# Attention and Mish FFN on one core: a pair's softmax straight behind its scores, other places for sums and x steps

## The chip, the core and the metric

The kernel runs on one core of one Trainium2 chip. The metric is the device time of one execution in microseconds (us). The core has TensorE (PE, with its weight loads shown apart as PEld), VectorE (DVE), ScalarE (ACT), GpSimd (POOL) and SyncE (SP, which issues nearly all DMAs here). Each takes its own instructions in order.

## The reference

Attention inside chunks of 64 tokens, for 8 heads of 64 columns, then a feed-forward network of 512 to 2048 to 512 over all 4608 tokens, in float32:

```
scores = scale * q_c @ k_c^T ;  scores -= max(scores)
attn   = exp(scores) / (sum(exp(scores)) + 1e-09)
x      = attn @ v_c                    # heads side by side: (4608, 512)
h      = x @ w_in
g      = h * tanh(softplus(h))         # Mish; softplus(h) = h over 20
out    = g @ w_out
```

## The kernel before

Tokens are worked in 18 pairs of 256. Two pairs make a first block of 512 tokens, which runs by itself; the other 16 make four blocks m = 1 to 4 of 1024 tokens, and while block m is in the network, the attention of the four pairs of block m + 1 is done beside it. The products of the network are done by a scheme of Winograd's kind: seven products of quarter matrices instead of eight, with sums of the parts of x (`x_step`: T1 to T4), of w_in (S1 to S4) and of w_out (T1 to T4, made by `t_whole`, `t_sums`, `t_hi`, `t_lo`, `t_store`; called T-matrices here, u = 0 to 7). Each float32 factor is split into a high part of fewer bits and the rest, and three matmuls are done for one.

All order is written by hand (`tc.manual_schedule()`); the order of the calls is the order of each engine's and queue's instructions. Tiles come from rings of buffers, so an instruction also waits until the former user of its buffer is done.

Block 1 runs in `unit` and then `phase_two` (L1140), 16 steps f = 0 to 15 of 12 matmuls: each casts gh on ACT, subtracts gl on DVE (`g_split`), and `X_PACE[f]` x steps follow. At f = 1 it does the scores and maxima of block 3's first pair (`scores_apart`, `max_apart`), at f = 2 the differences (`sub_apart`).

Blocks 2 to 4 (BOTH_FROM = 2 up to QUADS = 4) run in two stages.

First stage, `up_two(m, n)` (L1240) for n = 0 to 3: the pair with number j of block m + 1 is worked beside 14 products, seven kinds k for two units u; h = 2 * k + i counts them from 0 to 13. A product is 6 matmuls of 128 x 512. Behind each product stand its copies, additions and Mish (G11, G12, G21, G22), then `beside(h)` (L1247) with the steps of the attention and of the sums. Products 8 and 9 (k = 4) are copied by ACT at L1307, and products 10 and 11 (k = 5) write the same banks. The attention of a pair: `scores_apart`, `max_apart`, `sub_apart` (in the pair before, at h = 12, 12, 13), `a_exp` (h = 0), `a_inverse` (sums and reciprocals, h = 2), `a_norm` (3), `a_turn` (transposition on DVE, 4), `a_place` and four `a_swap` (copies on ACT, 5 to 9), `a_values` (matmuls with v, 12), `a_raw` (three copies, 12). v comes in four DMAs of 128 KB (`load_v`), q and k of the next pair in two of 512 KB (`load_qk`), on SP's queue with the loads of operands: 256 KB for each product, issued nine products ahead (`load_op`). In block 2 `BUILDS_UP` adds the T-matrices 4 to 7 at places (n, h).

Second stage, `down_all(m)` (L1344): seven types k of eight steps, 56 steps of 12 matmuls. A step makes the operand of the step after next (`operand`: gh cast on ACT at L1329, gl on DVE at L1332), and the sum of one kind (`difference`, `s_one`, `s_three`); in the first four steps after a type one part of its output is copied and added (`keep_wide`, `total_wide`, DVE at L1389), and one x step of the 22 is taken from `todo`. The accumulator banks are X (two banks, and X_a in the bank that the values of the attention use), Y and Z.

The lines that set the places before:

```
1248  at_ = (5, 6) if m == BOTH_FROM else (1, 2)     # s_sums: sums of g, two units
1329  nc.scalar.copy(out=d["gh"], in_=g)
1332  nc.vector.tensor_tensor(out=d["gl"], in0=g, in1=d["gh"].bitcast(F32), op=ALU.subtract)
1449  if k in (2, 4, 5) and todo:
1450      todo.pop(0)()
```

Of the kernel before, what the change touches and what calls it, by code (L numbers as in the profile page):

```python
# [24 lines left out]
def kernel(  # L25
# [1000 lines left out]
    for n in range(NU):  # L1026
        BUILDS_DOWN.setdefault(n + 1, []).append((t_keep, n))
    BUILDS_UP = t_plan(
        (4, [(0, h) for h in (4, 5, 6, 7, 10)]),
        (5, [(0, 8), (0, 10), (0, 11), (1, 1), (1, 5)]),  # L1030
        (6, [(1, h) for h in (4, 7, 10, 11, 13)]),
        (7, [(2, h) for h in (7, 8, 11, 11, 13)]),
    )

    def unit(m, u):
# [104 lines left out]
    def phase_two(m):  # L1140
        after = m < QUADS
        p = first_pair(m)
        todo = []
        if after:
            todo = [lambda n=n: x_step(m + 1, 0, n) for n in range(len(X_STEPS))]
            todo += [lambda: a_raw(first_pair(m + 1) + 3)]
            todo += [lambda n=n: x_step(m + 1, 1, n) for n in range(len(X_STEPS))]
        for f in range(NF):
            d = {}
            if f == 0:  # L1150
                filled(12)
            g_split(d, z_of(f), f"{m}b_{f}", True)
            if f == 0:
                for t in range(TOK // P):
                    filled(3)
                    store(f"{m}a", (p, p + 2), t)
            elif after or f < NF - 1:
                filled(12)
            down((m, 1), f, d)
            for _ in range(X_PACE[f]):  # L1160
                if todo:
                    todo.pop(0)()
            if m == BOTH_FROM - 1:
                run(BUILDS_DOWN, f)
            nxt = first_pair(m + 2)
            if f == 1:
                a_values(nxt - 1)
                scores_apart(nxt, ("h", "h"))
                max_apart(nxt)
            if f == 2:  # L1170
                sub_apart(nxt)

# [61 lines left out]
    def s_sums(u):  # L1236
        s_one(u)
        s_three(u)

    def up_two(m, n):  # L1240
        units = (2 * n, 2 * n + 1)
        xt, yt, vt = flip(m)
# [2 lines left out]
        x, y, v_ = {}, {}, {}  # L1245

        def beside(h):  # L1247
            at_ = (5, 6) if m == BOTH_FROM else (1, 2)
            if h in at_ and n:
                s_sums(2 * n - 2 + at_.index(h))  # L1250
            if m == BOTH_FROM:
                run(BUILDS_UP, (n, h))
            if h in (10, 11) and n == NU // 2 - 1:
                ready.append(operand(0, h - 10))
            if not on:
                return


            if h == 0:
                a_exp(j)  # L1260
            if h == (1 if n else 3):
                load_v(j)
            if h == 2:
                a_inverse(j)
            if h == 3:
                a_norm(j)
            if h == (3 if n else 5) and first_pair(m + 1) + n + 1 < first_pair(QUADS + 1):
                load_qk(j + 1, pool=(ob_p, "ob"))
            if h == 4:
                a_turn(j)  # L1270
            if h == 5:
                a_place(j)
            if h in (6, 7, 8, 9):
                a_swap(j, h - 6)
            more_ = n < 3 or m + 1 < QUADS
            if h == 12:
                a_values(j)
                if more_:
                    scores_apart(j + 1, yt if n < 3 else ("h", "h"))
                a_raw(j, None if n < 3 else ob_p)  # L1280
                if more_:
                    max_apart(j + 1)
            if h == 13 and more_:
                sub_apart(j + 1)

        for k in range(7):
            for i, u in enumerate(units):
# [56 lines left out]
    def down_all(m):  # L1344
# [83 lines left out]
        for i, (k, u) in enumerate(steps_):  # L1428
# [17 lines left out]
            if late:  # L1446
                step, t = late.pop(0)
                step(t)
            if k in (2, 4, 5) and todo:
                todo.pop(0)()  # L1450
            if u == NU - 1 and k in ends_wide:
                late += [(ends_wide[k], t) for t in range(4)]
# [74 lines left out]
```

## Time and profile before

| | |
|---|---|
| time, median of 3 runs (lowest to highest) | 795.51 us (795.15 to 797.99) |
| the profiled execution | 794.95 us, its span 792.9 us |
| PE busy | 774.7 us, 98% |
| PEld busy | 645.1 us, 81% |
| DVE busy | 574.9 us, 73% |
| ACT busy | 500.6 us, 63% |
| DMA | 245 GB/s in the mean |
| granted clock of PE | 1.0 throughout |

The span holds block 2's stages from 299.6 to 387.4 and to 467.2, block 3's to 553.6 and 634.1, block 4's to 710.4 and the end. PE's idle time is small everywhere but at the start, so the busy share tells little; the waits of PE by stretch tell what is left. A wait names the line that waited and, behind the arrow, the line that it waited for. For one wait the row of a matmul and that of its weight load differ, since a matmul's recorded end lies beyond the start of the next one, and weight loads run ahead.

### The profile page before, as it was taken

How to read it: one execution, taken by the hardware profiler on the slowest of the kernel's cores; microseconds unless marked ns; L12 is line 12 of the kernel's file. 1: busy time of each engine (PE TensorE's matmuls, PEld its weight loads, DVE VectorE, ACT ScalarE, POOL GpSimd, SP SyncE). 2: the span in 40 equal slices, each digit the busy share in tenths (PEclk: the TensorE clock that was granted, in tenths of full speed). 3: DMA queues.
4: the chain of work that ended last, by engine and by line, in shares of the span. 5: the costliest groups of instructions: out<-in, count | busy, mean ns of one | idle time of the engine just before them, and what ended most of it. 6: DMA issues, size and time to landing. Idle time of an engine off the chain costs nothing.

```text
span 792.9 us, 15588 instructions
## 1 busy us (share of the span) xinstructions
PE 774.7 (98%) x5850; PEld 645.1 (81%) x5850; DVE 574.9 (73%) x917; ACT 500.6 (63%) x787; POOL 2.2 (0%) x7
## 2 busy tenths in 40 slices
PE   5999999999999999999999999999999999999998
PEld 4887887888788887788888888887888888888887
DVE  6778898755757886777799965565899823348875
ACT  5988986736547447787756657777556444454443
POOL 1000000000000000000000000000000000000000
PEclk9999999999999999999999999999999999999999
DMA  9889989777687958998767688776676776766774
GB/s 335 306 316 319 331 307 337 231 229 279 204 285 230 298 193 256 328 342 297 237 187 215 178 260 265 244 242 205 175 213 187 229 222 191 197 193 188 215 192 129
DMA packets 100235, 193.97 MB, mean 245 GB/s; under 512 B 10561, under 2 KB 25921, under 8 KB 98113
## 3 DMA queue, kind: packets, MB, share of 16 engines
q1 hardware_dynamic: 99552, 192.19, 76.4%
q8 instruction: 47, 0.77, 0.4%
q10 hardware_dynamic: 608, 0.79, 0.3%
q14 instruction: 28, 0.22, 0.1%
HBM read 149.95 MB, written 42.99 MB: 243 GB/s over the span
## 4 chain that ended last, share of the span: by engine, by line
PE 85%; DVE 7%; ACT 4%; DMA 2%; issue 2%; SPq 0%; ACTq 0%; DVEq 0%
PE x L987 19%; PE v L987 10%; PE X_a L1373 8%; PE X L1373 8%; PE Z L1373 6%; PE y L987 5%; PE o L690 5%; PE Y L1373 4%; PE h L652 4%; PE av L388 2%; PE s L349 1%; PE o_(1, 1)_0_2775 L690 1%; DVE gl L1332 1%; PE o_(1, 0)_1_1662 L690 1%; PE o_(1, 1)_1_2779 L690 1%
## 5 line engine op out<-in xcount | busy, mean ns | idle before, releaser
L1329 ACT CAST gh<-g 128x512 fp32r<-128x512 f32 x168 | 103.6, 621 | 86.1 <-PE X_a L1373 47.0
L1332 DVE TENSOR_TENSOR gl<-g,gh 128x512 fp32r<-128x512 f32 x168 | 114.6, 686 | 29.9 <-ACT gh L1329 29.0
L987 PE MATMUL x<-x_T,w 128*128 128x512 f32 x366 | 91.0, 391 | 1.3 <-ACT g L1307 1.3
L987 PEld LDWEIGHTS x<-x_T,w 128*128 128x128 f32 x366 | 68.2, 188 | 17.0 <-ACT g L1307 2.5
L1000 DVE TENSOR_TENSOR g<-v,g 128x512 f32<-128x512 f32 x48 | 33.0, 690 | 64.9 <-ACT g L1307 44.1
L665 ACT ACTIVATE g<-g 128x512 f32<-128x512 f32 x72 | 45.4, 633 | 46.0 <-DVE g L1000 44.8
L652 PE MATMUL h<-x_first,wi 128*128 128x512 f32 (+1 forms) x216 | 47.2, 370 | 1.3 <-ACT x_first L574 1.0
L987 PE MATMUL x<-x_T,late 128*128 128x512 f32 x186 | 45.6, 391 | 0.5 <-DMA late<-wa 0.3
L652 PEld LDWEIGHTS h<-x_first,wi 128*128 128x128 f32 x216 | 37.0, 188 | 8.2 <-issue 1.1
L987 PEld LDWEIGHTS x<-x_T,late 128*128 128x128 f32 x186 | 34.7, 188 | 8.8 <-ACT g L1307 1.0
L690 PE MATMUL o<-wo,gh 128*128 128x512 f32 x128 | 39.5, 390 | 0.0
L1373 PE MATMUL X<-w,gh 128*128 128x512 f32 (+1 forms) x114 | 34.4, 384 | 0.0
L1373 PE MATMUL X_a<-w,gh 128*128 128x512 f32 (+1 forms) x114 | 34.2, 382 | 0.0
L987 PE MATMUL v<-x_B,w 128*128 128x512 f32 x126 | 32.8, 397 | 0.2 <-issue 0.2
L1000 DVE TENSOR_TENSOR g<-y,g 128x512 f32<-128x512 f32 x24 | 16.1, 670 | 22.9 <-PE y L987 20.2
L987 PE MATMUL y<-x_B,w 128*128 128x512 f32 x126 | 32.0, 397 | 0.0
L987 PE MATMUL x<-x_B,w 128*128 128x512 f32 x126 | 31.2, 389 | 0.0
L511 ACT COPY ps<-p 32x512 f32<-32x512 f32 x48 | 29.7, 618 | 0.9
L1373 PE MATMUL Z<-w,gh 128*128 128x512 f32 x108 | 29.5, 394 | 0.0
L690 PEld LDWEIGHTS o<-wo,gh 128*128 128x128 f32 x128 | 24.0, 188 | 4.8
L987 PEld LDWEIGHTS v<-x_B,w 128*128 128x128 f32 x126 | 23.0, 188 | 6.0 <-issue 0.7
L987 PEld LDWEIGHTS y<-x_B,w 128*128 128x128 f32 x126 | 23.1, 188 | 5.7 <-DVE zb L1000 0.9
(216 smaller groups left out, 1799.0 us busy)
## 6 DMA issues: line engine op xcount, KB each, us to landing
w<-wa SPq DMA_DIRECT2D x142, 256.0 KB, 4.0
w<-wb SPq DMA_DIRECT2D x94, 256.0 KB, 2.9
late<-wa SPq DMA_DIRECT2D x74, 256.0 KB, 3.1
late<-wb SPq DMA_DIRECT2D x74, 256.0 KB, 2.8
wst<-in_w_in SPq DMA_DIRECT2D x16, 512.0 KB, 5.8
wst<-in_w_out SPq DMA_DIRECT2D x16, 512.0 KB, 5.6
v<-in_v SPq DMA_DIRECT2D x48, 128.0 KB, 4.4
wa<-a SPq DMA_DIRECT2D x6, 1024.0 KB, 4.2
```

What stands on the lines that cost most here:

```text
L349: nc.tensor.matmul(o[c][rows_of(c ^ t), n], lhsT=d["q"][rows_of(c), t, n], rhs=d["k"][rows_of(c), t, n], start=True, stop=True,)
L388: nc.tensor.matmul(o[rows_of(h), c ^ t, t, g].rearrange("p (i k) -> p i k", i=2), lhsT=d["v"][rows, c, n], rhs=d["ps"][rows, :, c, n], sta ...
L511: nc.scalar.copy(out=d["ps"][to, 1 - i].rearrange("p c n k -> p (c n k)"), in_=d["p"][of, i].rearrange("p c n k -> p (c n k)"),)
L652: nc.tensor.matmul(h[:, cols], lhsT=wi[i // 2][:, i % 2 * 2 + kt // 2, w_, kt % 2], rhs=x[:, x_, kt, cols], start=(n == 0), stop=(n == 3 * ...
L665: nc.scalar.activation(out=out_, in_=in_, func=AF.Mish)
L690: nc.tensor.matmul(acc[t], lhsT=g[:, t * P : (t + 1) * P], rhs=wo[f // 2][:, f % 2, part], start=(f == 0 and n == 0), stop=(f == NF - 1 an ...
L987: nc.tensor.matmul(o, lhsT=t[:, w_, kt], rhs=x[x_][:, kt], start=(start and i == 0), stop=(i == 5), skip_group_check=not start,)
L1000: nc.vector.tensor_tensor(out=z, in0=o, in1=z, op=ALU.add)
L1329: nc.scalar.copy(out=d["gh"], in_=g)
L1332: nc.vector.tensor_tensor(out=d["gl"], in0=g, in1=d["gh"].bitcast(F32), op=ALU.subtract)
L1373: nc.tensor.matmul(o, lhsT=d[g][:, t * P : (t + 1) * P], rhs=w__, start=(first and n == 2), stop=(u == NU - 1 and g == "gl"), skip_group_c ...
```

## The change

It moves instructions; it neither adds nor removes any.

- `a_exp` of the next pair goes from the pair's product 0 to directly behind its differences: in `phase_two` at f = 2, in `up_two` at h = 11 of the pair before. Sums and norm go to h = 0, the turn to 1, the place copy to 3, the swaps to 4, 5 and 6 (two), and values, next scores, raw copies, maxima and differences from 12 and 13 to 11.
- In the first pair of block 2, v is loaded after product 4 instead of 3 and q, k of the next pair after 2 instead of 5; the other first pairs keep 3 and 5.
- The sums of g (`s_sums`) go to h = 7 and 8 in all blocks, from 5 and 6 in block 2 and 1 and 2 in blocks 3 and 4.
- The steps of T-matrices 4 to 7 get other places; the steps of T-matrix 5 that stood in the second pair (low half and store) go to the end of the first, its high half behind the raw copies.
- In `down_all` x steps are taken at types 0 (six), 2 (last four), 4 (eight) and 5 (last four) instead of 2, 4 and 5 (eight, eight and six).

```diff
--- before.py
+++ after.py
@@ -1026,10 +1026,10 @@
     for n in range(NU):
         BUILDS_DOWN.setdefault(n + 1, []).append((t_keep, n))
     BUILDS_UP = t_plan(
-        (4, [(0, h) for h in (4, 5, 6, 7, 10)]),
-        (5, [(0, 8), (0, 10), (0, 11), (1, 1), (1, 5)]),
-        (6, [(1, h) for h in (4, 7, 10, 11, 13)]),
-        (7, [(2, h) for h in (7, 8, 11, 11, 13)]),
+        (4, [(0, h) for h in (4, 5, 9, 10, 11)]),
+        (5, [(0, 6), (0, 8), (0, "raw"), (0, 13), (0, 13)]),
+        (6, [(1, h) for h in (4, 6, 9, 10, 11)]),
+        (7, [(2, h) for h in (4, 6, 9, 10, 11)]),
     )
 
     def unit(m, u):
@@ -1169,6 +1169,7 @@
                 max_apart(nxt)
             if f == 2:
                 sub_apart(nxt)
+                a_exp(nxt)
 
 
 
@@ -1237,6 +1238,8 @@
         s_one(u)
         s_three(u)
 
+    S_AT = (7, 8)
+
     def up_two(m, n):
         units = (2 * n, 2 * n + 1)
         xt, yt, vt = flip(m)
@@ -1245,9 +1248,8 @@
         x, y, v_ = {}, {}, {}
 
         def beside(h):
-            at_ = (5, 6) if m == BOTH_FROM else (1, 2)
-            if h in at_ and n:
-                s_sums(2 * n - 2 + at_.index(h))
+            if h in S_AT and n:
+                s_sums(2 * n - 2 + S_AT.index(h))
             if m == BOTH_FROM:
                 run(BUILDS_UP, (n, h))
             if h in (10, 11) and n == NU // 2 - 1:
@@ -1257,31 +1259,33 @@
 
 
             if h == 0:
-                a_exp(j)
-            if h == (1 if n else 3):
+                a_inverse(j)
+                a_norm(j)
+            if h == 1:
+                a_turn(j)
+            if h == 3:
+                a_place(j)
+            if h in (4, 5):
+                a_swap(j, h - 4)
+            if h == 6:
+                a_swap(j, 2)
+                a_swap(j, 3)
+            if h == (1 if n else 4 if m == BOTH_FROM else 3):
                 load_v(j)
-            if h == 2:
-                a_inverse(j)
-            if h == 3:
-                a_norm(j)
-            if h == (3 if n else 5) and first_pair(m + 1) + n + 1 < first_pair(QUADS + 1):
+            if h == (3 if n else 2 if m == BOTH_FROM else 5) and j + 1 < first_pair(QUADS + 1):
                 load_qk(j + 1, pool=(ob_p, "ob"))
-            if h == 4:
-                a_turn(j)
-            if h == 5:
-                a_place(j)
-            if h in (6, 7, 8, 9):
-                a_swap(j, h - 6)
             more_ = n < 3 or m + 1 < QUADS
-            if h == 12:
+            if h == 11:
                 a_values(j)
                 if more_:
                     scores_apart(j + 1, yt if n < 3 else ("h", "h"))
                 a_raw(j, None if n < 3 else ob_p)
+                if m == BOTH_FROM:
+                    run(BUILDS_UP, (n, "raw"))
                 if more_:
                     max_apart(j + 1)
-            if h == 13 and more_:
-                sub_apart(j + 1)
+                    sub_apart(j + 1)
+                    a_exp(j + 1)
 
         for k in range(7):
             for i, u in enumerate(units):
@@ -1446,7 +1450,7 @@
             if late:
                 step, t = late.pop(0)
                 step(t)
-            if k in (2, 4, 5) and todo:
+            if todo and ((k == 0 and u < 6) or k == 4 or (k in (2, 5) and u >= 4)):
                 todo.pop(0)()
             if u == NU - 1 and k in ends_wide:
                 late += [(ends_wide[k], t) for t in range(4)]
```

## Rows read from the trace of the kernel before

**Rows 1.** Busy time by stretch, start:end, length, engines' us (instructions), clock, DMA share, GB/s

```profile
299.60:387.40 87.80, 86.44 (x851) 70.28 (x849) 63.49 (x93) 69.39 (x105) 0.00 (x0) 1.00 0.93 309
387.40:467.20 79.80, 79.27 (x449) 68.31 (x448) 73.43 (x135) 44.68 (x84) 0.00 (x0) 1.00 0.70 201
```

**Rows 2.** Waits of PE's matmuls, 299.6 to 634.1: us in total, times, longest

```profile
PE x L987 <- ACT g L1307: 1.5, 4, 0.8
PE Z L1373 <- DVE gl L1332: 1.0, 4, 0.3
PE X_a L1373 <- ACT late L553: 1.0, 1, 1.0
```

**Rows 3.** The same for PE's weight loads

```profile
PEld x L987 <- ACT g L1307: 3.5, 5, 1.2
PEld Z L1373 <- DVE gl L1332: 2.7, 4, 0.8
PEld X_a L1373 <- ACT late L553: 1.8, 2, 1.5
```

**Rows 4.** Chain that ended last, pieces that begin a pair: start, us, what

```profile
299.62 2.72 PE x L987 x12
323.10 2.73 PE x L987 x12
344.63 2.72 PE x L987 x12
365.92 2.72 PE x L987 x12
488.51 2.74 PE x L987 x12
```

**Rows 5.** Timeline of block 3's second pair: start, us, engine, line [idle before, releaser]

```profile
490.53 1.28 ACT L445 ACT_TABLE_LOAD   x1
491.83 1.06 ACT L445 ACTIVATE p<-p 128x1024 f32<-128x1024 f32 x1
494.65 1.21 DVE L470 TENSOR_REDUCE r<-p 128x16 f32<-128x1024 f32 x1
499.35 1.05 ACT L502 COPY ps<-p 128x1024 f32<-128x1024 f32 x1 [0.81 <-DVE p L497]
501.71 0.58 ACT L1307 COPY g<-x 128x512 f32<-128x512 f32 x1
```

**Rows 6.** Timeline of DVE in block 2's second stage, type 5

```profile
451.10 0.68 DVE L1332 TENSOR_TENSOR gl<-g,gh 128x512 fp32r<-128x512 f32 x1
452.49 0.68 DVE L607 TENSOR_TENSOR x_T<-late,x_T 128x512 fp32r<-128x512 f32 x1
453.09 0.68 DVE L1332 TENSOR_TENSOR gl<-g,gh 128x512 fp32r<-128x512 f32 x1
```

**Rows 7.** Timeline of phase two of block 1, its fourth step

```profile
261.57 0.62 ACT L674 CAST gh_1b<-zb 128x512 fp32r<-128x512 f32 x1 [4.36 <-PE o_(1, 1)_3_2787 L690]
261.77 1.28 DVE L372 TENSOR_TENSOR p<-s,m 128x512 f32<-128x512 f32 x2
262.97 0.68 DVE L680 TENSOR_TENSOR gl_1b<-zb,gh_1b 128x512 fp32r<-128x512 f32 x1
264.09 0.39 PE L690 MATMUL o_(1, 1)_0_2775<-wo,gl_1b 128*128 128x512 f32 x1
```

**Rows 8.** Block 2's first pair: timeline; DMA issues (KB each, median us landing)

```profile
307.43 2.86 SPq L311 DMA_DIRECT2D v<-in_v  x4
313.78 0.38 SPq L300 DMA_DIRECT2D late<-in_k  x1
318.90 1.16 PE L388 MATMUL av<-ps,v 64*64 64x64 f32 x64
...
v<-in_v SPq DMA_DIRECT2D x4, 128.0 KB, 6.4
late<-in_k SPq DMA_DIRECT2D x1, 512.0 KB, 5.8
```

## The prediction

> **What bounds the kernel now.** I read the busy table by stretch first [rows 1]: TensorE (PE) is busy 86.44 of 87.80 us in the first stage of block 2 and 79.27 of 79.80 in its second. The kernel is bound by PE's own matmuls, and the change alters none of them. It can only win back idle time of PE, and only from where the diff reaches: late in block 1 to the end of block 3 (block 4 has no attention and no x steps, and PE waits for nothing there). The second view is PE's waits over that stretch [rows 2], the third those of its weight loads [rows 3]. A wait shows twice: the matmul row is short, as modelled ends of matmuls cover a part; the weight-load row is long, as a weight load normally runs ahead. The loss lies between. I take two thirds of the way up, because the chain of work by pair [rows 4] shows a loss of 0.24 in a pair where no matmul waits: pairs of block 2 begin at 299.62, 323.10, 344.63 and 365.92, so the third takes 21.29, the second 21.53, the first 23.48.
>
> Three waits matter. I number a pair's 14 products 0 to 13, as h does in the code. **L1307**: PE waits for ScalarE's (ACT's) copies of products 8 and 9, 1.5 to 3.5, say 2.8 in all; of that the longest, 0.8 to 1.2 (1.1), is in block 2's first pair. **L553**: the second stage's accumulator X_a waits for the copies of the last pair's values, 1.0 to 1.8, say 1.5. **gl**: PE waits for VectorE's (DVE's) low half of g in the second stages, 1.0 to 2.7, say 2.1. Together 6.4 us, 0.8%, the most that the change can win, but for 1.1 more that the first pair of block 2 loses (2.2 against the third) and that these rows don't explain.
>
> **L1307, part by part.** ACT and DVE work in order. In block 3's second pair [rows 5] the exp runs at 491.83, 3.3 us into the pair (PE starts it at 488.51 [rows 4]), the sums at 494.65, the place copy waits for the transpose till 499.35, two swaps follow, and L1307 starts only at 501.71. The change issues the exp in the pair before, directly behind its scores, and the sums at the pair's first product. Exp then: scores end 2.2 behind product 11, maxima and differences 2 x 1.28 on DVE (row of the differences in rows 7; the maxima taken as equal), so differences end 4.8 and exp (1.06) 5.9 behind product 11; the next pair starts 2.2 + 2 x 1.36 = 4.9 behind it (a product is half of the 2.72 that a row of 12 matmuls takes [rows 4]). DVE first does two additions of 0.6, so the sums begin 1.2 us into the pair instead of 6.1. The place copy no longer waits for DVE but for its turn on ACT, which I work out as 7.3 to 8.4 us in, against 10.8 to 11.9 now; swaps end by 11.9; L1307 can start at product 8's end, 12.4. The wait was about 0.5 and the work is 3.5 earlier: gone in block 3. Win 2.8 - 1.1 = 1.7 outside block 2's first pair. In block 2's second pair the low half of T-matrix 5 (1.2 us of DVE, now at product 13) pushes the sums to 2.4 us in; L1307 is then ready 0.1 to 0.3 late, cost 0.2. Switches between the exp and the Mish tables stay two per pair. One costs 1.28, and exp starts 0.02 behind it [rows 5].
>
> The Trainium skill ("ScalarE: Activation LUTs", What ACT_TABLE_LOAD costs) adds a drain of about 1.38 us to each switch, which would speak against putting exp between Mish steps. This trace disagrees: 490.53 + 1.28 = 491.81, and exp starts at 491.83.
>
> **X_a.** The last pair's values move one product (1.36) forward, and their copies now follow the Mish of product 11, which reads PE's bank, instead of one that waits for DVE. They end about 1 us ahead of X_a. Win 1.5.
>
> **x steps and sums of g and w_out.** In the second stage DVE makes one gl per step of PE; an operation of 512 columns takes 0.60 from start to start, a pair of output additions 0.79 [rows 6]. A step lasts 79.27 / 56 = 1.41 [rows 1]. With gl, x step and output pair DVE needs 1.99 per step, 0.58 too much, for four steps at the start of type 2 and of type 5; DVE is busy 73.43 of 79.80 in all. That is the gl wait. Now six x steps go to type 0 (gl, x: 1.20; eight steps hold 8 x 0.60 + 6 x 0.60 + 3 sums of 0.60 = 10.2 of 11.3) and types 2 and 5 get theirs after the output pairs are done (1.20). No type but 1 (0.6 over, within the two steps that operands are made ahead) exceeds PE. Win 2.1. The sums at products 7 and 8 and the T-steps fall where DVE has 2 to 3 us free; they cost nothing on PE's path except as said below. No queue of POOL is passed.
>
> **New wait 1, end of block 1.** exp of the next pair now stands in ACT's queue behind step 2 of phase two. There DVE ends the differences at 263.05, and ACT cast the next gh at 261.57, ahead of that [rows 7]. Now that gh waits: differences 263.05, exp 1.06, gh 0.62, gl 0.68 make 265.4; PE wants gl at 264.09. Behind the exp nothing else waits for long. Cost 1.4, with 1.2 to 1.6 as bounds.
>
> **New wait 2, first pair of block 2.** The SP queue issues q and k (1 MB) now after product 2, v after product 4; before it was v after 3 and q, k after 5. v's four issues at 307.43 and on land 6.4 later, k is issued at 313.78 and lands 5.8 later, at 319.6, just ahead of its use, and values start at 318.90 [rows 8]. With the L1307 wait (1.1) gone and values one product (1.36) sooner, PE would be there at 316.4. The same transfers minus one operand (256 KB; at the stage's 309 GB/s [rows 1] 0.85 us) must land first: 318.8. PE waits 2.4. Bounds: the queue is 93% busy; if it makes up that 7% of 16 us, 317.7; if q, k and an operand (1.3 MB, 4.2 us) simply add to v's present 316, 320.2. So 1.3 to 3.8. I take 2.4, since the same transfers have been timed as a set. The pair ends at 318.8 + 2.2 + 2.7 = 323.7 against 323.10: all effects of this pair together cost 0.6 (-0.5 to 2.0), the 1.1 of L1307 included.
>
> **New wait 3, end of block 2's first stage.** Here the next pair's scores go to the banks that products 10 and 11 fill, and they come one product sooner, right behind 11. Counted from product 11's end: the second L1307 ends at -2.0, the sums at product 8 hold DVE's addition behind it till -0.9, ACT then does Mish, Mish, gh, Mish at 0.6 each and frees the bank at 1.5; values end at 1.1. PE waits 0.5 (0 to 0.8). Then scores end at 2.7, maxima and differences at 5.2, exp at 6.3, Mish table at 7.6, two Mish at 8.8, and only then gh of the second stage's third operand, at 9.4. PE starts that stage at 2.7 + 2 x 1.36 = 5.4 and its third step at 8.2: it waits 1.2 (0.5 to 1.6). Both have no cover: PE has nothing else in its queue.
>
> **Sum.** Won: 1.7 + 1.5 + 2.1 = 5.3. Lost: 0.2 + 1.4 + 0.6 + 0.5 + 1.2 = 3.9. Net 1.4 us. The profiled execution took 794.95 (span 792.9 and 2.05 around it), 0.56 under the median of 795.51. It would come to 793.5; put on the median, 794.1.
>
> **Rivals.** (1) The new waits of block 2 fall away: loads use the queue's idle share or the transfers are faster in the new order, and the tail's ACT work is hidden. For it: 7% idle DMA share, k landing only a moment late now; against: [rows 8], the queue landed v and k 6 us after issue. Time 794.1 - 2.4 - 1.2 = 790.5. (2) Slower: the load queue. If v lands behind q and k at the late bound, and the second pair's v, q, k are pushed by the 1 MB store of T-matrix 5, which now stands ahead of them on SP and keeps it till that low half is made, the waits of block 2 grow; the sign turns when v lands later than 318.8 + 1.4 = 320.2. With 2 us more in the first pair and 2 in the second, 798.1. For it: 93% share; against: transfers ease later in the stage. (3) The gl wait only moves, since sums of g and x steps now meet in type 0: the 2.1 are not won, 796.2. Against: 10.2 of 11.3 us there. (4) The copy of L1307 stays late, as ACT's work, not DVE's, holds it: 794.1 + 1.7 = 795.8. Against: 3.5 us of room. (5) A switch of tables holds ACT for longer than its 1.28, with no instruction to show it: at twice that, the two switches at block 2's end add 2.6, 796.7. Against: the 0.02 us behind a switch in rows 5. By "ScalarE: Activation LUTs" of the Trainium skill (section as above) it would be 2 x 1.38 more, an estimate of 796.9.
>
> **How the numbers follow.** Forecast 0.53, rival 1 0.2, rival 2 0.12, rival 3 0.08, rival 4 0.05, rival 5 0.02. The forecast's own bounds (phase two 0.2, first pair -1.1 to 1.4, block 2's end -1.2 to 0.7) give 792 to 796. The range takes in rivals 1 and 3 to 5 and most of 2: 790.3 to 797.6. What a measurement of this kernel tells from no change is about 0.5%, 4.0 us: faster means under 791.5, slower over 799.5. Faster: nearly all of rival 1, 0.2. Slower: the far part of rival 2, 0.06. Within: 0.74.
>
> **What would show it.** Of after: PE's rows on L1307 and L553 gone in block 3, the gl rows gone in both second stages; a new PE wait for gl_1b near 264; a PE wait at the first values of block 2 for a load, with v landing near 320 (1.4 later by wait 1); one at scores for ACT's Mish and one for gh (not gl) in the third step near 392. If none of the last three shows, rival 1 holds; if block 2's first two pairs take over 25 us, rival 2. I am wrong altogether if PE's own matmul time changes.

## The result and the profile after

| | before | after |
|---|---|---|
| median (lowest to highest), us | 795.88 (794.11 to 798.36) | 800.53 (796.16 to 807.12) |
| ratio, 95% interval | | 1.0055 (1.0031 to 1.0078) |
| profiled execution, us | 794.95 | 807.12 |
| its span, us | 792.9 | 805.3 |

The changed kernel is slower by half a per cent, 4.4 us by the ratio; the forecast was 1.4 us faster, 794.1, with a range up to 797.6. The profiled execution of after is the longest of its thirteen, so its trace overstates the loss. A second execution of the same kernel (e1_again, below; span 797.5) lies near the median, and I use both.

I cut each trace at the first matmul of every stage and pair, as the timeline of TensorE (PE) gives it, and compare lengths. That table carries most of what follows (us; "again" is e1_again, and the columns to the right of it are experiments):

| stretch | before | after | again | e2 | e3 | e4 | e10 | e5 | e11 |
|---|---|---|---|---|---|---|---|---|---|
| up to phase two | 253.56 | 259.02 | 255.34 | 254.31 | 258.49 | 254.06 | 255.14 | 254.72 | 254.49 |
| phase two of block 1 | 45.89 | 47.41 | 47.37 | 45.89 | 47.37 | 47.37 | 47.37 | 45.90 | 45.89 |
| block 2, pair 1 | 23.49 | 25.73 | 25.14 | 25.30 | 21.85 | 25.07 | 25.33 | 22.61 | 23.21 |
| pair 2 | 21.52 | 21.29 | 21.32 | 21.33 | 22.61 | 21.29 | 21.31 | 22.09 | 21.50 |
| pair 3 | 21.29 | 23.20 | 21.35 | 23.18 | 22.85 | 23.19 | 22.62 | 22.63 | 21.29 |
| pair 4 | 21.32 | 22.78 | 22.33 | 22.09 | 22.09 | 22.07 | 22.09 | 21.68 | 21.32 |
| block 2, second stage | 79.95 | 82.59 | 81.05 | 80.90 | 82.59 | 78.56 | 79.79 | 78.81 | 78.73 |
| block 3, four pairs | 85.85 | 85.45 | 85.49 | 84.41 | 85.49 | 84.33 | 86.07 | 86.17 | 85.60 |
| block 3, second stage | 81.09 | 78.56 | 78.56 | 78.56 | 78.56 | 78.56 | 78.56 | 78.56 | 78.56 |
| rest | 158.87 | 159.25 | 159.54 | 159.23 | 159.31 | 158.91 | 159.44 | 159.43 | 158.89 |

Two things are read off first. The stretch up to phase two is the same code in all nine (but for one small fill in e10), and it lasts from 253.56 to 259.02: 5.5 of the 12.4 us between the two spans arise before anything that the change moved. And in the code that the diff touches there are gains (both second stages, block 3's pairs where nothing else happens) and losses (phase two, block 2's pairs, the start of its second stage); the losses are larger.

PE's waits in the kernel after from 255 us on, the view that answers [rows 2] (us in total, times, longest; gl_1b is the low half gl of a step of phase two, av the values, s the scores, and "issue" means that the profile shows nothing that was waited for):

```profile
PE s L349 <- issue: 2.8, 3, 1.5
PE X L1377 <- ACT gh L1333: 2.2, 1, 2.2
PE av L388 <- DMA v<-in_v: 2.1, 2, 1.5
PE o_(1, 1)_0_2775 L690 <- DVE gl_1b L680: 1.2, 1, 1.2
PE s L349 <- ACT g L665: 0.4, 1, 0.4
```

The three rows of [rows 2] are gone, all of them. Four waits that the prediction named have come: for v, for gh, for gl_1b, and, at `s L349 <- ACT g L665`, for the bank of the scores. The first row was not named: in it PE waits for nothing that the profile shows, three times inside the 64 matmuls of a pair's scores. Before, the like happened once, in block 2's first pair:

```profile
PE v L987 <- issue: 0.2, 1, 0.2
```

By that matmul it is 0.2; from the row ahead of it to the next one it is 0.63. Together with a wait of 0.3 for an operand (`late<-wa`, at 306.71) that is up to 0.9 of the 1.1 us which the prediction could not explain in that pair.

The windows of block 2's pairs and second stage, and of block 3's second stage, answer to [rows 1]. Columns as there:

```profile
306.43:332.16 25.73, 23.51 (x213) 19.18 (x212) 16.84 (x24) 15.19 (x25) 0.00 (x0) 0.93 0.96 306
332.16:353.45 21.29, 21.29 (x213) 17.65 (x212) 17.49 (x25) 16.32 (x27) 0.00 (x0) 1.00 0.99 326
353.45:376.65 23.20, 21.69 (x213) 17.85 (x212) 16.86 (x25) 16.83 (x27) 0.00 (x0) 1.00 0.86 293
376.65:399.43 22.78, 21.83 (x213) 17.92 (x212) 14.18 (x22) 16.70 (x28) 0.00 (x0) 1.00 0.71 232
399.43:482.02 82.59, 80.35 (x449) 70.00 (x448) 73.08 (x134) 48.39 (x86) 0.00 (x0) 0.98 0.69 197
567.46:646.02 78.56, 78.56 (x449) 68.69 (x448) 72.34 (x133) 44.59 (x83) 0.00 (x0) 1.00 0.73 208
```

Block 3's second stage is pure PE: busy 78.56 of 78.56. Block 2's is longer by 4.03 for the same 449 matmuls (a step of this stage is eight matmuls, four of 512 columns and four of 256, and not twelve; 56 steps make 448), though PE waits only 2.24 there, and its busy time is longer too (80.35): the granted clock is 0.98, not 1.00. The first pair shows the same, 0.93. In slices of 2 us around the wait for v (ahead of 326) and the wait for gh (402 to 404.6) it is plain:

```profile
322.00:324.00 2.00, 1.45 (x7) 0.87 (x7) 0.74 (x2) 1.23 (x2) 0.00 (x0) 1.00 1.06 236
324.00:326.00 2.00, 0.49 (x17) 0.35 (x21) 1.23 (x1) 1.32 (x3) 0.00 (x0) 1.00 1.05 311
326.00:328.00 2.00, 2.00 (x100) 2.00 (x93) 0.00 (x0) 0.67 (x2) 0.00 (x0) 0.58 1.05 386
328.00:330.00 2.00, 2.00 (x40) 1.75 (x35) 0.96 (x2) 1.41 (x3) 0.00 (x0) 0.56 1.10 428
330.00:332.00 2.00, 2.00 (x11) 1.60 (x10) 2.00 (x4) 0.40 (x1) 0.00 (x0) 1.00 0.69 274
...
402.00:404.00 2.00, 0.38 (x4) 0.17 (x2) 0.00 (x0) 1.99 (x4) 0.00 (x0) 1.00 0.60 176
404.00:406.00 2.00, 1.38 (x4) 1.09 (x5) 1.40 (x3) 2.00 (x5) 0.00 (x0) 0.71 0.23 86
406.00:408.00 2.00, 2.00 (x8) 1.75 (x7) 2.00 (x4) 1.69 (x4) 0.00 (x0) 0.50 0.00 0
408.00:410.00 2.00, 2.00 (x12) 1.72 (x11) 2.00 (x4) 0.62 (x1) 0.00 (x0) 0.94 0.49 131
```

Behind each of the two waits the clock is at 0.50, the 1.2 GHz level, for between 3 and 4 us (the shares of the slices together), and then back at 2.4 GHz. With the clock at 0.50 the slice of 406 to 408 holds 8 matmuls where the slices from 410 to 420, at full clock, hold 13 or 14. It doesn't follow every time: in e1_again the same wait for gh, 2.24, ends at 398.03 and is followed by a clock of 1.00,

```profile
398.00:400.00 2.00, 1.97 (x11) 1.71 (x12) 1.99 (x4) 2.00 (x5) 0.00 (x0) 1.00 0.04 16
```

and the stage takes 81.05 instead of 82.59. So the wait costs 81.05 - 78.56 = 2.5 with what stands around it, and the fall of the clock, where it comes, 1.5 more.

The chain of the wait for gh, on ScalarE's (ACT's) timeline (start, us, line, idle before and releaser), answers to [rows 5]:

```profile
395.86 0.40 ACT L553 COPY late<-av 128x256 f32<-128x256 f32 x1
399.26 1.28 ACT L445 ACT_TABLE_LOAD   x1 [3.00 <-DVE p L372]
400.55 1.06 ACT L445 ACTIVATE p<-p 128x1024 f32<-128x1024 f32 x1
401.62 1.28 ACT L665 ACT_TABLE_LOAD   x1
402.91 1.15 ACT L665 ACTIVATE g<-g 128x512 f32<-128x512 f32 x2
403.96 0.60 ACT L1333 CAST gh<-g 128x512 fp32r<-128x512 f32 x1
```

ACT is idle for 3.00 us and then loads the table of exp: the load itself stands behind the wait for the differences (DVE p L372). The forecast let exp begin when the differences end. (L665 is Mish, with its own table; L1333 is the cast of gh that PE waits for.) In phase two the same load did not wait: it runs at 262.70 and exp 5.85 later, when the differences are there:

```profile
262.70 1.28 ACT L445 ACT_TABLE_LOAD   x1
268.55 1.06 ACT L445 ACTIVATE p<-p 128x1024 f32<-128x1024 f32 x1 [4.57 <-DVE p L372]
```

The waits for instructions: one of the three, in the third pair of block 2, as the timeline of PE shows it:

```profile
370.88 0.53 PE L349 MATMUL s<-late 64*64 64x64 f32 x20
372.92 0.92 PE L349 MATMUL s<-late 64*64 64x64 f32 x44 [1.51 <-issue]
```

### The profile page after: what moved, and what is told of

Its sections match the earlier page's. It is cut to its first block, busy times and chain, and to the rows that moved or that the text cites. A ratio compares the mean times of both kernels' runs of the same rounds, so it can differ in the third digit from the quotient of the medians.

```text
span 805.3 us, 15579 instructions
## 1 busy us (share of the span) xinstructions
PE 779.6 (97%) x5850; PEld 652.8 (81%) x5850; DVE 577.0 (72%) x917; ACT 497.4 (62%) x787; POOL 2.3 (0%) x7
## 4 chain that ended last, share of the span: by engine, by line
PE 87%; ACT 4%; DMA 4%; DVE 3%; issue 2%; SPq 0%; ACTq 0%; DVEq 0%
PE x L987 20%; PE v L987 10%; PE X L1377 8%; PE Z L1377 8%; PE X_a L1377 8%; PE y L987 6%; PE Y L1377 4%; PE h L652 4%; PE o L690 3%; DMA wst<-in_w_in 2%; PE s L349 2%; PE av L388 2%; PE o_(1, 0)_1_1662 L690 1%; PE o_(1, 0)_2_1666 L690 1%; PE o_(1, 0)_3_1683 L690 1%
## 5 line engine op out<-in xcount | busy, mean ns | idle before, releaser
L1333 ACT CAST gh<-g 128x512 fp32r<-128x512 f32 x168 | 103.9, 620 | 88.8 <-PE X_a L1377 49.1
L665 ACT ACTIVATE g<-g 128x512 f32<-128x512 f32 x72 | 44.4, 630 | 40.2 <-DVE g L1000 39.6
L1311 ACT COPY g<-x 128x512 f32<-128x512 f32 x24 | 14.1, 587 | 23.5 <-PE x L987 23.3
```

The source lines that it names most:

```text
L665: nc.scalar.activation(out=out_, in_=in_, func=AF.Mish)
```

## What I took it to be, and the rivals

My theory after the result: the loss is made of four things that the change puts before PE, of which the first three can be taken out alone. (a) Phase two: exp ahead of a gh of the same stage. (b) Block 2's first pair: v behind q and k on the load queue. (c) Block 2's end: exp, with its two table loads, ahead of the gh of the second stage. (d) Waits of PE for its own instructions, in the bursts of small matmuls. The parts a to c should add up to the loss and more, since the rest of the change gains what was forecast.

Rivals: that the change's gain isn't there, the second stages being shorter for another reason; and, for d, that such a wait belongs to a place in the program (the semaphores or buffers of the scores) and not to the stream of instructions.

### after again (e1_again)

The kernel after, unaltered.

> The changed kernel once more, unaltered, to see which of the losses repeat. Theory A (named waits): in every execution of it PE waits about 1.4 us for gl_1b in block 1's phase two, 2 to 2.5 us for v in the first pair of block 2, and about 2.2 us for gh in the third step of block 2's second stage, and its clock falls to 0.5 for some 3 us behind the last two; the time stays 2.5 to 6 us over the kernel before. Theory B (the loss is mostly PE running out of instructions, rows 'issue' inside the 64 x 64 matmuls, 3.4 us in the first trace against 0.24): these rows are at the same places with the same lengths. If B's rows move or vanish while the time stays, A carries the loss. The 5.5 us that the first trace lost ahead of any changed instruction should be gone if it was of that execution alone.

Measured: 799.55 (797.34 to 802.89), ratio 1.0048 (1.0030 to 1.0066). Of the 5.5 us ahead of phase two 1.8 are left. The waits for v, gh and gl_1b and the bank came again, that for v shorter (1.1) and none with a fall of the clock behind it, which the first expectation had wrong; the wait for instructions did not come at the same places: none in the third pair, but one of 1.59 right behind the first pair's burst:

```profile
321.20 1.10 PE L388 MATMUL av<-ps,v 64*64 64x64 f32 x59 [1.13 <-DMA v<-in_v]
...
327.38 0.63 PE L987 MATMUL v<-x_B,w 128*128 128x512 f32 x2 [1.59 <-issue]
```

### exp of phase two one step later (e2_exp_later)

```diff
             if f == 2:
                 sub_apart(nxt)
-                a_exp(nxt)
+            if f == 3:
+                a_exp(nxt)
```

> The changed kernel, but the exp of the next pair stands one step later in phase two of block 1, behind the gh cast of the fourth step. Theory A: the wait for gl_1b (1.2 in PE's row, 1.6 in the weight load's) is gone, nothing else there waits, and the time is 1.4 us under the changed kernel's. Rival: DVE, not ACT's queue, is what is late there, as it has no idle time from the maxima to the differences; then a wait of at least 1 us stays in the fourth or fifth step.

Measured: 798.4, ratio 1.0026 (1.0012 to 1.0041). Phase two is back at 45.89 and nothing is late behind it. Against 1.0052, the mean of the two measurements of after, 0.0026 come back, 2.1 us, for 1.5 in the trace; the intervals of the two overlap.

### loads and values of block 2's first pair as before (e3_first_pair)

```diff
-            if h == (1 if n else 4 if m == BOTH_FROM else 3):
+            if h == (1 if n else 3):
                 load_v(j)
-            if h == (3 if n else 2 if m == BOTH_FROM else 5) and ...
+            if h == (3 if n else 4 if m == BOTH_FROM else 5) and ...
                 load_qk(j + 1, pool=(ob_p, "ob"))
...
-            if h == 11:
+            if h == (12 if n == 0 and m == BOTH_FROM else 11):
                 a_values(j)
```

> The changed kernel, but in block 2's first pair alone the values, next scores, raw copies, maxima, differences and exp come after product 12 instead of 11, and v is loaded after product 3 and q, k after 4 instead of 4 and 2. Theory A: the wait for v (2.1 to 2.5) and the clock's fall behind it (about 1.9 more) are gone; a wait of 0 to 0.8 for q and k may take its place; the pair takes 22 to 23 us instead of 25.7, the time is 3 to 4 us under the changed kernel's. Rival: the loads' total is what bounds this pair; then PE waits for q and k as long as it did for v and the pair still takes over 25.

Measured: 798.38, ratio 1.0026 (1.0003 to 1.0048), 2.1 us under after where 3 to 4 were expected; the interval overlaps with that of after, so the trace carries this one. The first pair falls from 25.14 and 25.73 to 21.85, so it is 1.6 shorter than before too; the clock stays at 1.00 in it and v lands 5.2 us after its issue, not 7.2 (the pair's window in e3, v's issues in after and in e3):

```profile
305.86:327.71 21.85, 21.58 (x214) 17.57 (x212) 15.74 (x23) 14.49 (x25) 0.00 (x0) 1.00 0.98 316
...
v<-in_v SPq DMA_DIRECT2D x4, 128.0 KB, 7.2
...
v<-in_v SPq DMA_DIRECT2D x4, 128.0 KB, 5.2
```

A part moves: the second pair takes 22.61 instead of 21.3 (PE there waits 0.4 and 0.3 for ACT's copies of x, L1304 and L1311).

### exp of block 3's first pair within the second stage (e4_exp_in_stage2)

```diff
                     sub_apart(j + 1)
-                    a_exp(j + 1)
+                    if n < 3:
+                        a_exp(j + 1)
...
+            if k == 6 and u == 0 and not last and m + 1 < QUADS:
+                a_exp(nxt + 4)
```

> The changed kernel, but the exp of block 3's first pair, which stood behind block 2's last scores, is done at the start of the last type of block 2's second stage. Theory A: the wait for gh in the third step (2.2 in PE's row) and the clock's fall behind it (about 1.7) are gone, the wait of 0.4 of the scores for ACT's Mish stays; the time is 3.5 to 4 us under the changed kernel's. Rival: the table switches hurt wherever they stand; then gh or gl makes PE wait 1 us or more in the last type instead.

Measured: 796.49, ratio 1.0005 (0.9994 to 1.0017): 0.0047 come back, 3.7 us, the most of the three, and the interval lies clear of that of after. The second stage of block 2 takes 78.56, as block 3's, with the clock at 1.00; the wait for the bank (0.46) stays.

```profile
393.05:471.61 78.56, 78.56 (x449) 68.66 (x448) 72.50 (x134) 47.05 (x85) 0.00 (x0) 1.00 0.73 204
```

### the table of exp loaded ahead (e10_table_ahead)

The disputed 1.28 by itself. The exp stays where the change put it, and an exp of one column, of a tile of its own, goes ahead of the maxima:

```diff
+                if more_ and n == 3:
+                    nc.scalar.activation(out=tiny, in_=tiny, func=AF.Exp)
                 if more_:
                     max_apart(j + 1)
                     sub_apart(j + 1)
                     a_exp(j + 1)
```

> The kernel after with one more activation of a single column (Exp, on a tile of its own that nothing reads) ahead of the maxima in block 2's last pair, so that ScalarE loads the table of exp while VectorE still makes the differences. Theory that the gh wait came out 1.0 longer than forecast because the load of 1.28 stands behind the exp's wait for VectorE: the load moves to some 3 us earlier, the exp begins within 0.1 of the end of the differences, gh's wait falls from 2.24 to 0.9 to 1.1, the clock behind it stays up or falls for a shorter time; second stage of block 2 from 81.1 to 82.6 down to 79.5 to 80. Total 1.3 to 3 us under the kernel after. Rival, that the wait is set by the length of the two tables' work or by the differences themselves: the wait stays over 2 us and the total is that of after.

ACT's timeline at the same place as above (the lines of this kernel are numbered two to four higher):

```profile
391.43 1.28 ACT L1288 ACT_TABLE_LOAD   x1
392.72 0.20 ACT L1288 ACTIVATE tiny<-tiny 128x1 f32<-128x1 f32 x1
393.69 1.06 ACT L447 ACTIVATE p<-p 128x1024 f32<-128x1024 f32 x1 [0.77 <-DVE p L374]
394.76 1.28 ACT L667 ACT_TABLE_LOAD   x1
```

and PE's wait behind it:

```profile
PE X L1381 <- ACT gh L1337: 1.0, 1, 1.0
```

The wait fell from 2.24 to 1.0 and the stage from 81.05 in e1_again to 79.79, both with the clock at 1.00: the load's 1.28, to a tenth. The rival expectation (over 2) is out. The total, 799.05, ratio 1.0034 (1.0018 to 1.0050), lies by the ratios 1.1 us under e1_again and 1.7 under the first measurement of after, at the low end of what I expected or under it; the intervals overlap, so the total alone would not have shown it.

### 60 and 166 instructions more ahead of everything (e6_60_more, e7_166_more)

To test d: the kernel after with 30 and 83 tiny matmuls at its start, each a weight load and a matmul in PE's stream.

```diff
     with tc.manual_schedule():
+        idle["h"] = ps_h.tile([P, TOK], F32, name="unread", tag="h")
+        for _ in range(30):
+            nc.tensor.matmul(idle["h"][0:32, 0:16], lhsT=ones[:, 0:32], rhs=ones[:, 0:16], start=True, stop=True)
         first_block()
```

> The kernel after with 30 tiny matmuls (32 rows, 16 columns) ahead of everything, 60 instructions more in TensorE's stream; nothing else. They cost 1 to 2 us at the start, beside the first loads, so 0 to 2 us of the total. Theory that the issue waits are TensorE's instructions coming late in pieces of 256: the places where a piece ends move 60 instructions earlier, out of the back of the burst in block 2's third pair (from 171 to 110 of some 256 instructions in) and in its fourth pair from 244 to 183, so the issue waits stand at other instructions of TensorE (60 earlier in the kernel's own count, 194 modulo 256 of the whole stream), and the 1.5 us in the third pair gets smaller or goes, while another burst may get one. Rival, that an issue wait belongs to the place in the program (the values and scores themselves, their semaphores, the queues at that time): the waits stay at the same matmuls, 1.5 us in the third pair of block 2. Total by the first: 0.3 to 2 us under the kernel after plus the start; by the rival: equal to it or up to 2 us more.

> The kernel after with 83 such tiny matmuls ahead of everything, 166 instructions more. Theory of pieces of 256: in block 2's third pair a piece now ends 5 instructions into the burst of values and scores and the next one at its end, so that a whole piece is used up in some 2.2 us and the next one has to come in that time: an issue wait of 1.5 us or more just behind that burst; in the fourth pair (78 in) and the second (188 in) smaller ones or none. Rival (place in the program): the same waits as in the kernel after. The start costs 1 to 4 us beside the first loads by both.

I numbered the rows of PE and of its weight loads (PEld), those of the sequencer that issues both among them, by their starts, from 0. Numbers of the rows, in or right behind a burst of values and scores, that start 0.9 us or more behind the row ahead of them while PE waits for nothing that the profile shows:

| kernel | number in the stream | the same, less the added ones |
|---|---|---|
| after | 6337, 8641 | 6337, 8641 |
| after again | 5569 | 5569 |
| e2, e4 | 5569, 6337 | 5569, 6337 |
| e3 | 6337 | 6337 |
| e10 | 5569, 6337, 8641 | 5569, 6337, 8641 |
| e5 | 6337, 8641 | 6337, 8641 |
| e11 | 8641 | 8641 |
| e7 (166 more) | 6081, 8385 | 5915, 8219 |
| e8 (e5 with 60 more) | 9153 | 9093 |
| e6 (60 more) | none | |

Every one of these numbers leaves 193 when divided by 256. So do, in the twelve traces other than e9's, all 22 such waits behind 150 us that are over 0.4 from row to row, the one of the kernel before (5569) among them. Without added instructions they are three places of the program; with them none of the three has a wait, and new places have one, again at 193. That is what the theory of pieces of 256 says, and it excludes the rival. The trace shows the pieces: the queue named instruction moved 47 packets, 0.77 MB, in the whole span, 16 KB each, and PE's 12,123 rows, those of its sequencer among them, make 47.4 times 256. In the kernel after, between the two ends of pieces around the third pair (360.26 and 372.92), the queue's rows in the stretches 360.3 to 370.3 and 370.3 to 372.9 are

```profile
q1 hardware_dynamic: 1745, 3.22, 92.8%
...
q1 hardware_dynamic: 326, 0.58, 66.0%
q8 instruction: 1, 0.02, 2.3%
```

so for 10 us no piece came, and the one that did (its packet took from 370.49 to 371.44) let PE go on at 372.92, 1.5 later. In the kernel before, the stretch of 341.6 to 351.5, one piece long as well, has two:

```profile
q1 hardware_dynamic: 1342, 3.22, 89.9%
q8 instruction: 2, 0.03, 1.4%
```

My expectation for e7 was wrong in one respect: I had the wait in the third pair, where a piece ends 5 instructions into the burst, and it came in the second, 188 in, and in block 3's first:

```profile
346.78 0.46 PE L349 MATMUL s<-late 64*64 64x64 f32 x15
348.93 0.80 PE L349 MATMUL s<-late 64*64 64x64 f32 x35 [1.69 <-issue]
```

In the third pair the next piece's packet began 0.2 us behind the end of the last one, and the burst, which used the piece up in 2.6 us, waited for only 0.4 (the pair took 21.67). What sets how soon that packet comes (0.2 to 10 us in block 2's pairs, in after and e7) I did not find.

The times: e6 801.11, ratio 1.0061 (1.0038 to 1.0083); e7 807.89, 1.0138 (1.0115 to 1.0161), with waits for v of 3.9 in the first pair, 2.9 the longest, and issue waits of 3.6 in all. So 60 instructions that do nothing left the time where it was, though the profile, of the shortest of e6's six executions, has no long wait for instructions left in it: the total expected of e6, under that of after but for the start, did not come, and what d is worth in the total is not shown. 166 cost 6.8 us against the mean of after. The trace of e7 shows where: block 2's first pair took 27.41, its second 23.33 and block 3's first 25.14, against 25.14, 21.32 and 22.45 in e1_again. The clock fell to 0.50 behind three waits there, one of them a wait for instructions (1.94, then 0.50 from 500 to 502). That v came later there than in after is shown; why 166 idle instructions ahead of everything do that is not.

### before with the x steps alone (e9_before_pace)

```diff
-            if k in (2, 4, 5) and todo:
+            if todo and ((k == 0 and u < 6) or k == 4 or (k in (2, 5) and u >= 4)):
```

> The kernel before with one part of the change alone: x's steps in the second stages at other places (the last edit of the diff). Theory by the rows: the waits of TensorE for gl go in the second stages of blocks 2 and 3, each some 1.2 us shorter (before 79.95 and 81.09), all else as before: 793.4 (ratio 0.997, 0.9955 to 0.999). Rival, that the gl waits were covered by others that end later: 796, ratio 1.000, the stages within 0.4 of before.

Measured: 794.41, ratio 0.9980 (0.9965 to 0.9994): 1.6 us won where 2.1 were forecast; the rival's 1.000 lies outside the interval. The trace has a granted clock of 0.86 over the whole span and is not compared; the times alone are used.

### block 3 on, without block 2's pairs and phase two (e11_block_3_on)

```diff
             if f == 2:
                 sub_apart(nxt)
-                a_exp(nxt)
...
+            if m == BOTH_FROM:
...
+                return
...
+            if k == 6 and u == 0 and not last and m + 1 < QUADS:
+                a_exp(nxt + 4)
```

The lines left out in the middle are the steps of the kernel before, word for word; the sums of g and the T-steps are back at their old places too.

> The kernel after with phase two and all four pairs of block 2 as in the kernel before (softmax, loads, sums of g and sums of w_out back at their old places), with the exp of block 3's first pair at the start of the last type of block 2's second stage. So the change acts in the second stages, and in blocks 3 and 4, alone. Theory that the change's loss is made in phase two and block 2's pairs and its gain elsewhere: phase two 45.9, pairs of block 2 23.5, 21.5, 21.3, 21.3 as before, second stages 78.6 each, block 3's pairs 21.3, 21.3, 21.3, 20.4: 5 us under the kernel before, ratio 0.9935 (0.992 to 0.996). Rival, that the waits for instructions eat this wherever they fall: 2 us of it lost in bursts of values and scores, ratio 0.996 to 0.998, no better than e5.

Measured: 792.40 (789.67 to 795.59), ratio 0.9953 (0.9936 to 0.9969). PE's longest waits from 299 us on:

```profile
PE x L987 <- ACT g L1340: 0.9, 1, 0.9
PE s L349 <- issue: 0.8, 1, 0.8
```

The first is the copy of product 8 in block 2's first pair, here as before. So the part of the change that acts from block 2's second stage on, with the exp of block 3's first pair placed as in e4 (neither as before nor as in the change), is worth 3.7 us (2.5 to 5.1) where 5 were expected; block 3's pairs took 85.60 against 84.33 in e4, with an issue wait of 0.8 in the second. What the change does in phase two, in block 2's pairs and with that exp is all of the loss. The rival's 0.996 lies within the interval and is not excluded. This version and e8 below are the fastest measured; their intervals overlap.

### all mends together (e5_all_mended, e8_mended_60_more)

The exp of phase two as in e2, loads as in e3, exp of block 3's first pair as in e4, and in block 2's first and last pair the next scores, maxima and differences at product 12; e8 is e5 with the 30 tiny matmuls.

> The kernel after with four mends together: the exp of phase two one step later (as e2), the values' load back at product 3 and the next pair's q and k at product 4 in block 2's first pair (as e3), the next scores, maxima and differences of block 2's first and last pair back at product 12 (the values stay at 11), and the exp of block 3's first pair at the start of the last type of block 2's second stage (as e4). Theory that the change's loss is the waits it puts before TensorE plus the half clock behind them: phase two 45.9 instead of 47.4, first pair 21.8 instead of 25.7 or little more, second stage of block 2 78.6 instead of 82.6, the wait of the scores for the bank (0.46) gone, so 5 to 8 us under the kernel after, 792 to 794, ratio to the kernel before 0.996 (0.994 to 0.998). Rival, that TensorE's waits for nothing that the profile shows ("issue" waits) are the larger part and stay: they come in bursts of values and scores wherever the instruction count puts them; then 794 to 796 and ratio 0.998 to 1.000, with issue waits of over 1 us in the pairs.

> e5 with the 30 tiny matmuls of e6 ahead. Tells whether the places of the issue waits can be chosen in the mended kernel too: by the theory of pieces they move 60 instructions earlier against e5; the total lies within 2 us of e5, on the side that the sum of issue waits moves to. By the rival the waits are those of e5 and the total is e5's plus the start (0 to 2 us).

Measured: e5 794.41, ratio 0.9971 (0.9957 to 0.9986); e8 792.98, 0.9950 (0.9933 to 0.9968). Phase two 45.90, second stage 78.81, no wait for v, gh, gl_1b or the bank. The longest that are left in e5 from 255 us on:

```profile
PE s L349 <- issue: 1.8, 2, 1.0
PE v L987 <- issue: 0.4, 1, 0.4
PE x L987 <- ACT g L1316: 0.3, 1, 0.3
```

Both expectations held in part: with the waits of a to c gone the loss is gone, and waits for instructions, 2.2 us by these rows, are left in e5; that they are what keeps it from its lower bound is not shown. Block 2's pairs, 89.0 in all, are no shorter than in e11 (87.3). In e8 the waits moved, as expected, out of block 2's pairs to one of 1.3 in block 3; its time is nominally 1.4 below e5's, with intervals that overlap.

## Why the prediction was wrong

What the change was to win it won. What failed are two steps of the losses, the end of block 2's first pair and the exp at block 2's end, and two terms that the sum put at nothing without a reason: TensorE's clock behind a wait, and TensorE's waits for its own instructions.

**What held.** The waits on L1307, L553 and gl went, as the sum had them. Block 3's pairs: 84.33 in e4 against 85.85, 1.5 won (forecast 1.7 for L1307 outside block 2's first pair). Block 3's second stage: 2.53 won, block 2's in e11 1.22. If the gl waits cost the same in each, that is 2.4 for gl (forecast 2.1) and leaves 1.3 for X_a, whose wait stood in block 3's alone (forecast 1.5). In all 5.2 against 5.3. Rivals 3 and 4 are out, and rival 1 as well, since the new waits came.

**New wait 1** was 1.18 by the matmul's row, and phase two 1.5 longer; forecast 1.4 (its own rows give 265.4 - 264.09 = 1.3).

**New wait 2: the wait was right, what stands behind it was not.** v let the last part of the values start at 325.75, 19.3 us into the pair; the forecast was 318.8 - 299.62 = 19.2. The waits add up to 2.1; forecast 2.4. But the step "the pair ends at 318.8 + 2.2 + 2.7" failed: behind the wait came 6.4 us in after, with the clock at 0.58 and 0.56 in the next two slices, and 6.7 in e1_again, with 1.59 of waiting for instructions, instead of 4.9. So the pair cost 1.65 to 2.24 against before instead of 0.6, over the bound of 2.0 in the profiled execution. With the loads in their old order and the values at product 12 (e3) the pair won 1.6, of which the second gives 1.1 back.

**New wait 3: the term of gh was mis-sized.** The wait for the bank was 0.44 (0.5). The wait for gh was 2.24 against 1.2, out of its bounds of 0.5 to 1.6. The step was "maxima and differences at 5.2, exp at 6.3": it priced the exp at 1.06 from the end of the differences and let its table be there. It rested on [rows 5], where the load at 490.53 had come just when the differences ended, so that one could not see whether it had waited for them. In after's row ACT is idle for 3.00 and then loads; e10 takes the load out of the way, and 1.3 of the wait with it (2.24 to 0.96). Of the 4.03 lost in this stage in the profiled execution 2.5 are the wait with what stands around it and 1.5 the clock, if e1_again (81.05 at a clock of 1.00) is taken as the stage without its fall.

The Trainium skill ("ScalarE: Activation LUTs", What ACT_TABLE_LOAD costs) was cited for a drain behind each load. Again there is none: load at 399.26 for 1.28, exp at 400.55. Rival 5 is out in this form: the time was not hidden behind the load, it was the load, standing in another place.

**No term at all.** The sum priced an idle stretch of PE at its length. Two things come on top that no step had: the clock behind the long waits, and PE out of instructions, 2.8 in the trace of after, 1.6 in e1_again, 2.9 in e4. The trace of before has such a row in block 2's first pair (0.63 from row to row), where the prediction noted 1.1 us that its rows don't explain and left it at that.

The Trainium skill ("Runtime: NRT & Kernel Launch", Instruction fetch mechanics) says that instructions come in blocks of 16 KiB, 256 of them, and that crossing a block's end is mostly hidden, since instructions are issued more slowly than they are brought. This trace agrees with the block; at most of its 47 ends nothing waits, but behind that at 372.92 PE stood for 1.5 us, in a burst of 256 instructions in some 2.2 us, with DMA over 90% busy for the 10 us ahead.

**Which rival it was.** Rival 2, slower, 798.1, gave the load queue as the cause; v landed where the forecast itself had it, and block 2's second pair had no wait for loads (block 3's first had one for k, 0.9 in e1_again, 0.4 in e3), so that was not it; that its time comes near the measured one is luck. The forecast's direction turned on the size of the losses: forecast 3.9, and in the traces of e1_again and after phase two 1.5, block 2's first pair 1.65 to 2.24, its later pairs 0.9 to 3.1 (each against before), the start of its second stage 2.5 to 4.0 (against 78.56), block 3's pairs 1.1 (against e4): 7.6 to 12.

**Does it add up?** In ratios, from the mean of the two measurements of after, 1.0052: e2 gives 0.0026 back, e3 0.0026, e4 0.0047; together 0.0099, which would be 0.9953. Against e1_again alone, measured beside the three, it is 0.0022, 0.0022 and 0.0043; of the three only e4's interval lies clear of that of after, so the sum is as rough as e2 and e3 are. e5, which has the three in much the same form (its values stay at product 11), is at 0.9971, with waits for instructions left in it; e11 at 0.9953. What stays open is what decides when a piece of instructions comes and what those waits cost in the total, why the clock falls behind a wait in some executions and not in others, what the 0.4 to 0.7 us are by which the rest behind block 3 is longer in most kernels than in before, and how much of the medians' difference lies in the unchanged stretch up to phase two, whose length differs by up to 5.5 us between traces.

## What to carry to other kernels

When a step is moved ahead of another on an engine that works in order, count everything that goes with it in the queue, a table load above all, and from its worst place: behind the wait of the instruction that it serves. Where a moved step makes the bounding engine wait, price the wait and what comes behind it, here up to 1.5 us of half clock, and keep a change out of the stretches where nothing was idle to be won: the same change won 3.7 us from block 2's second stage on (e11) and, by subtraction from the 4.1 that it lost in all, lost twice that (3.7 + 4.1) in phase two, block 2's pairs and the exp behind them.

## What the runs showed of the hardware

PE stands still at the end of a piece of 256 of its instructions when the next one comes late: up to 1.9 us, at numbers that leave 193 by 256 in every trace that has such a wait. It goes on 1.2 to 1.6 us behind the end of the fetch's packet in all 22 cases (371.44 to 372.92 in after; 347.31 to 348.93 in e7). Small matmuls make this visible, as 128 of them with their weight loads use up a piece in some 2.2 us where one of the second stage's products lasts 21 (421.21 to 442.38 in after). Adding instructions that do nothing moves the places.

A table load can run 5.85 us ahead of its exp (262.70 and 268.55) or wait with it (399.26, idle for 3.00 before); what decides between the two is not shown. A tiny activation of the same function ahead brought it forward (391.43, with exp at 393.69, in e10).

The granted clock fell to 0.50 behind a wait of 2.24 in after and stayed at 1.00 behind the same wait in e1_again; which it is to be, no run here tells.
